# Preparation of the second weights and the stores of finished pair rows on GpSimd's DMA queue, splits in 512-column pieces

## The chip, the cores and the metric

One Trainium2 chip, one core. The time is device microseconds of that core for the whole program, the median of several runs of the same build. TensorE (PE) multiplies, VectorE (DVE), ScalarE (ACT) and GpSimd (POOL) do the elementwise work, and transfers between HBM and the on-chip memory are issued from three queues: SyncE's (SP), ScalarE's (ACT) and GpSimd's (POOL).

## The reference

Linear attention over 8 batches, 8 heads, 576 rows and 64 columns, then two feed-forward layers on the 4608 x 512 result:

```
q_s = softmax over columns of q;  k_s = softmax over rows of k
kv  = k_s^T v;  x = q_s kv                      # x: 4608 x 512
h   = x @ w_in;  x = max(0.01 * h, h) @ w_out           # 512 -> 2048 -> 512
h   = max(x @ w1, x @ w2, x @ w3);  out = h @ w_out      # 512 -> 768 -> 512
```

The weights arrive as 8-byte floats; the result is 4-byte floats.

## The kernel before

**Numbers.** Every multiplied matrix is kept as a high and a low part (two 4-byte tiles), and each product is three matmuls: high x high, high x low, low x high. A split is one ACT copy (the high part) and one DVE subtraction (the low part).

**Stages.** The 4608 rows are nine chunks of 512. Chunks 0 to 2 go through attention and the first layer in the ordinary way (to about 340 us; the attention of the later chunks is prepared beside it and goes on to about 640 us). Chunks 3 to 8 are taken as three pairs, with seven block products in place of eight (Winograd's form of Strassen's scheme), from about 340 to 900 us: for each pair, eight turns `t` make the hidden rows and add up the left half of the output (`out_a(i, 0, ...)`), then a second half of the pair adds up the right side (`out_a(i, 1, ...)`), and in each half the last step evicts four finished accumulators (`store_pair`, L941). The second layer does the same for four pairs, from about 900 us to the end.

**What runs beside the pairs.** The second layer's weights are prepared during the first layer's pairs: nine `ahead_unit`s (L270) and three `ahead_out`s (L304). Each loads two 512 KB blocks of 8-byte weights (L277, L310), converts them (`convert_ahead`, begins with an ACT `Abs` at L254), makes sums of quarters, splits (`split_ahead`, L263) and stores eight 256 KB parts (L222, L301) or two 512 KB blocks (L327). The first layer's weights are stored again in parts during the first 300 us (`stage_a`, L673; `sums_a`, L688). `background(step)` advances all of these a stage at a time between the matmuls of the pairs. Attention of the later chunks loads k, v and q on POOL's queue (L394, L439, L498) and takes the column maximum there (L437).

**What sets the order.** Each engine and each queue works strictly in order. A scheduler places the instructions by its own estimate of when each can begin, except those given to `pin` (`tc.keep_in_program_order`): pinned instructions of an engine keep the order in which the program was written. SP's queue carries the pairs' weight loads (`group` from `stream_in`, L858; `outw` from `stream_out`, L870), which are pinned too.

**The finished rows.** `store_pair` copies one accumulator to an `st` tile on ACT (L943) and stores its two halves with two 128 KB transfers that ACT itself issues (L945): four accumulators, eight stores per half of a pair, 48 in all. The four `st` buffers are shared with the snapshots of the pairs' products (`snap_a`, L965).

Of the kernel before, what the change touches and what calls it, by code (L numbers as in the profile page):

```python
# [9 lines left out]
F32R = mybir.dt.float32r  # L10
U32 = mybir.dt.uint32
I64 = mybir.dt.int64
AF = mybir.ActivationFunctionType
ALU = mybir.AluOpType
# [5 lines left out]
N = 512  # L20
# [14 lines left out]
H = N // 2  # L35
# [5 lines left out]
BEGUN = (0, 0, 0, 2, 3, 5, 7, 9, 11, 13, 15, 17, 19, 21, 23, 25)  # L41
# [29 lines left out]
def tile_kernel(ctx: ExitStack, tc: tile.TileContext, q, k, v, wa, wb, out):  # L71
# [12 lines left out]
    nc = tc.nc  # L84
# [6 lines left out]
    MA = wa.shape[0]  # L91
# [14 lines left out]
    def psum():  # L106
        return ps.tile([P, N], F32, tag="ps", name="ps")
# [10 lines left out]
    for i in range(4):  # L118
        z = slice(32 * i, 32 * i + 32)
# [18 lines left out]
    x2 = {t: dp.tile([P, KDM, N], F32, name=f"x2_{i}") for i, t in enumerate(turns)}  # L138
# [5 lines left out]
    pin = tc.keep_in_program_order  # L144
# [64 lines left out]
    CYCLE = len(USES) * NU  # L209

    stream = dp.tile([P, CYCLE + 3, 2, H], F32, name="stream")
    lone = [dp.tile([P, 2, H], F32, name=f"lone{i}") for i in range(NU)]
    ready_out = [dp.tile([P, 2, 2, N], F32, name=f"wo{t}") for t in range(MB // 2)]

    def place(part, u):

        return (u + (part in LATE)) % NU * len(USES) + USES.index(part)

    def to_stream(u, t, part):

        i = place(part, u)
        pin(nc.sync.dma_start(stream[:, i], t))  # L222
        if i < 3:
            pin(nc.sync.dma_start(stream[:, CYCLE + i], t))

    def sums_of_quarters(quarters, sums):
        a11, a12, a21, a22 = (quarters[:, i] for i in range(4))
        s2, s4, s1, s3 = (sums[:, i] for i in range(4))
        pin(nc.vector.tensor_tensor(s1, a21, a22, op=ALU.add))
        nc.vector.tensor_tensor(s2, s1, a11, op=ALU.subtract)  # L230
        nc.vector.tensor_tensor(s3, a11, a21, op=ALU.subtract)
        nc.vector.tensor_tensor(s4, a12, s2, op=ALU.subtract)
# [29 lines left out]

    def split_ahead(hi, z):  # L263

        pin(nc.scalar.activation(hi.bitcast(F32R), z, AF.Copy))
        pin(nc.vector.tensor_tensor(z.bitcast(F32R), z, hi, op=ALU.subtract))  # L266

    def two_rooms(t):
        return a_room(), a_room()

    def ahead_unit(u):

        t, j = UNITS[u]
        room, more = two_rooms(t)
        raw = room.bitcast(wb.dtype)[:, : 2 * N]
        for half in range(2):
            pin(nc.sync.dma_start(raw[:, half * N : half * N + N], wb[2 * t + half, j // 2, :, j % 2]))  # L277
        yield
        yield
        hi, whole = more[:, : 2 * N], more[:, 2 * N :]  # L280
        if wb.dtype == I64:
            for left in convert_ahead(raw, hi):
                if left is None:
                    yield
            nc.vector.tensor_tensor(whole, hi, left, op=ALU.add)
        else:
            nc.vector.tensor_copy(whole, raw)
        yield
        hi_sums, sums = room[:, : 2 * N], room[:, 2 * N :]
        sums_of_quarters(*(z.rearrange("p (b n) -> p b n", n=H) for z in (whole, sums)))  # L290
        yield
        split_ahead(hi, whole)
        split_ahead(hi_sums, sums)
        yield
        yield
        quarters, sums = (z.rearrange("p (h b n) -> p b h n", h=2, n=H) for z in (more, room))
        for i, part in enumerate(PARTS[:4]):
            if part in USES:
                to_stream(u, quarters[:, i], part)
            else:  # L300
                pin(nc.sync.dma_start(lone[u], quarters[:, i]))  # L301
        for i, part in enumerate(PARTS[4:]):
            to_stream(u, sums[:, i], part)

    def ahead_out(t):

        room, more = two_rooms(t)
        raw = room.bitcast(wb.dtype)[:, : 2 * N]
        for m in range(2):
            pin(nc.sync.dma_start(raw[:, m * N : m * N + N], wb[2 * t + m, 1, :, 1]))  # L310
        yield
        yield
        hi, z = more[:, : 2 * N], more[:, 2 * N :]
        if wb.dtype == I64:
            for left in convert_ahead(raw, z):
                if left is None:
                    yield
            nc.vector.tensor_tensor(z, z, left, op=ALU.add)
        else:
            nc.vector.tensor_copy(z, raw)  # L320
        yield
        split_ahead(hi, z)
        yield
        yield
        both_parts = more.rearrange("p (h m n) -> p m h n", h=2, m=2)
        for m in range(2):
            pin(nc.sync.dma_start(ready_out[t][:, m], both_parts[:, m]))  # L327

    wB = {}

# [343 lines left out]
    def stage_a(m):  # L674

        w = tiles[m].bitcast(F32)
        nc.sync.dma_start(stream_out[:, m], w[:, :, 1])
        i = m // 2 * len(AUSES)
        quarters = w[:, :, 0].rearrange("p h (b n) -> p b h n", n=H)
        for b in range(2):  # L680
            if m % 2 == 0:
                nc.sync.dma_start(stream_in[:, i + AUSES.index(("a11", "a12")[b])], quarters[:, b])
            elif b == 1:
                nc.sync.dma_start(stream_in[:, i + AUSES.index("a22")], quarters[:, b])
        yield
# [63 lines left out]

    def ahead_units():  # L750
        for m in range(MA):
            yield max(BEGUN[m] + 3, 8), stage_a(m)
        for t in range(MA // 2):
            yield (30, 34, 38, 42, 49, 53, 57, 61)[t], sums_a(t)
        for u, at in enumerate((66, 75, 84, 97, 105, 112, 119, 122, 128)):
            yield at, ahead_unit(u)
        for t, at in enumerate((92, 114, 131)):
            yield at, ahead_out(t)
        for c, at in enumerate((CONV * MA + len(APAIRS) * 2 * MA + 30, CONV * MA + len(APAIRS) * 2 * MA)):
            yield at, join(c)  # L760

    waiting = [u for c in range(2, NC) for u in plan_units(c)] + list(ahead_units())
    waiting.sort(key=lambda u: u[0])
    live = []
# [117 lines left out]
    for turn in turns:  # L882
        c = turn[0]
# [57 lines left out]
    def store_pair(i, side, f, acc):  # L941
        st = gp.tile([P, N], F32, tag="st", name="st", bufs=4)
        nc.scalar.activation(st, acc, AF.Copy)  # L943
        for at, c in enumerate(APAIRS[i]):
            pin(nc.scalar.dma_start(x2[c, 0, MA][:, f, side * H : side * H + H], st[:, at * H : at * H + H]))  # L945

    def out_a(i, side, t, f, pairs, ms=(0, 1)):

# [211 lines left out]
    for i in range(len(APAIRS)):  # L1160
# [6 lines left out]
        for t in range(MA // 2):  # L1167
# [4 lines left out]
            a, c = psum(), psum()  # L1172
# [176 lines left out]
```

## Time and profile before

| | us |
|---|---|
| three runs | 1459.7, 1455.17, 1457.37 |
| median | 1457.37 |
| the profiled execution | 1457.88 |
| its span | 1456.1 |
| PE busy | 1398.8 (96% of the span) |
| DVE, ACT, POOL busy | 874.2, 671.1, 90.2 |

A busy PE is not one at full speed: a matmul of 512 columns starts every 0.227 us when nothing holds it and the granted clock is full, and every 0.43 us at half of it. So lost time is found by counting matmuls in a stretch, not by the busy share alone.

### The profile page before, as it was taken

To read this page: it belongs to the slowest core of one execution; us is meant where nothing else is said; L and a number is where in the kernel's file an instruction comes from. 1 tells how busy PE (TensorE), PEld (TensorE's weight loads), DVE (VectorE), ACT (ScalarE), POOL (GpSimd) and SP (SyncE) were. 2 spreads that over 40 slices of the span, in tenths; PEclk is the share of its full clock that TensorE was granted. 3 is DMA by queue.
4 is the path that set the end of the run, shared out by engine and by line. 5 is a ranking of instruction groups with operands and counts; after the bars stand their busy time and mean duration, and the time that the engine had idled before them with its cause. 6 is when DMAs were issued, how large, how long until landed. Compare 5 with 4: busy or idle time off the path is not lost.

```text
span 1456.1 us, 18203 instructions
## 1 busy us (share of the span) xinstructions
PE 1398.8 (96%) x6624; PEld 1135.5 (78%) x6624; DVE 874.2 (60%) x1407; ACT 671.1 (46%) x1361; POOL 90.2 (6%) x162
## 2 busy tenths in 40 slices
PE   6999999999999899998999959999999999999998
PEld 4688867887888687886888837888888888888887
DVE  8888978965687856755566624356356444535311
ACT  6756857744675636644354433223223323323211
POOL 1000212200111100000000000001000000000000
PEclk9999999999999999999999979999999999999999
DMA  9468764526988839668768796754484664364510
GB/s 371 151 243 297 260 233 148 194 98 240 353 288 316 310 138 339 250 249 324 287 231 329 285 378 217 267 188 166 167 312 157 223 253 160 123 253 150 204 51 37
DMA packets 118809, 336.39 MB, mean 231 GB/s; under 512 B 11584, under 2 KB 59456, under 8 KB 96704
## 3 DMA queue, kind: packets, MB, share of 16 engines
q1 hardware_dynamic: 99904, 290.01, 54.5%
q0 software_dynamic: 9600, 34.73, 7.2%
q10 hardware_dynamic: 9216, 10.49, 2.1%
q8 instruction: 52, 0.85, 0.2%
q14 instruction: 37, 0.30, 0.1%
HBM read 256.80 MB, written 78.38 MB: 230 GB/s over the span
## 4 chain that ended last, share of the span: by engine, by line
PE 88%; DMA 4%; DVE 3%; ACT 2%; issue 2%; SPq 1%; ACTq 0%; POOL 0%; DVEq 0%; POOLq 0%
PE ps L847 39%; PE acc L620 33%; PE ps L620 12%; PE ps L448 1%; PE ps L572 1%; DMA wo<-wo 1%; DMA outw<-stream_out 1%; DMA wo<-room 1%; PE ps L552 1%; DMA spare<-in_q_dram 1%; DMA lone<-room 0%; SPq L222 0%; DMA vt<-in_v_dram 0%; DMA stream<-room 0%; DVE room L266 0%
## 5 line engine op out<-in xcount | busy, mean ns | idle before, releaser
L847 PE MATMUL ps<-op,group 128*128 128x512 f32 x1512 | 352.1, 389 | 0.7 <-ACT snap L1068 0.7
L847 PEld LDWEIGHTS ps<-op,group 128*128 128x128 f32 x1512 | 283.7, 188 | 60.0 <-ACT snap L1068 1.1
L620 PE MATMUL acc<-ghi,outw 128*128 128x512 f32 x768 | 258.6, 404 | 27.4 <-ACT st L943 21.6
L847 PE MATMUL ps<-opA,group 128*128 128x512 f32 x1008 | 250.1, 393 | 2.2 <-ACT snap L968 2.1
L847 PEld LDWEIGHTS ps<-opA,group 128*128 128x128 f32 x1008 | 188.5, 188 | 44.1 <-ACT snap L968 3.8
L620 PEld LDWEIGHTS acc<-ghi,outw 128*128 128x128 f32 x768 | 147.8, 194 | 62.7 <-ACT st L943 24.1
L620 PE MATMUL acc<-glo,outw 128*128 128x512 f32 x384 | 153.5, 400 | 3.5 <-DVE glo L641 3.4
L620 PE MATMUL acc<-wo,h 128*128 128x512 f32 x558 | 135.4, 389 | 0.0
L620 PE MATMUL acc<-ghi,w 128*128 128x512 f32 x384 | 127.9, 395 | 0.7 <-ACT st L650 0.7
L620 PE MATMUL ps<-xhi,w 128*128 128x512 f32 x384 | 126.0, 394 | 1.2 <-ACT g L894 0.8
L1068 ACT ACTIVATE snap<-ps 128x512 f32<-128x512 f32 x108 | 61.7, 596 | 134.5 <-PE ps L847 134.1
L620 PEld LDWEIGHTS acc<-wo,h 128*128 128x128 f32 x558 | 104.7, 188 | 21.8
L1083 DVE TENSOR_TENSOR snap<-snap,ps 128x512 f32<-128x512 f32 x72 | 49.2, 685 | 110.5 <-ACT snap L1068 91.5
L641 DVE TENSOR_TENSOR glo<-g,ghi 128x512 fp32r<-128x512 f32 x102 | 69.7, 687 | 67.5 <-ACT ghi L640 67.1
L620 PEld LDWEIGHTS acc<-glo,outw 128*128 128x128 f32 x384 | 74.1, 193 | 20.9 <-DVE glo L641 5.3
L620 PEld LDWEIGHTS ps<-xhi,w 128*128 128x128 f32 x384 | 71.9, 188 | 17.7 <-ACT g L894 1.2
L640 ACT ACTIVATE ghi<-g 128x512 fp32r<-128x512 f32 x102 | 63.6, 630 | 46.2 <-DVE g L1272 27.3
L620 PEld LDWEIGHTS acc<-ghi,w 128*128 128x128 f32 x384 | 71.6, 188 | 17.0 <-ACT st L650 1.4
L641 DVE TENSOR_TENSOR glo<-right,ghi 128x512 fp32r<-128x512 f32 x48 | 33.1, 689 | 82.6 <-ACT ghi L640 82.4
L1092 ACT ACTIVATE h<-best 128x512 fp32r<-128x512 f32 x48 | 30.3, 631 | 100.2 <-DVE best L1085 99.8
L620 PE MATMUL acc<-glo,w 128*128 128x512 f32 x192 | 75.8, 395 | 0.5 <-DVE glo L641 0.5
L620 PE MATMUL ps<-xlo,w 128*128 128x512 f32 x192 | 75.1, 391 | 0.1
(171 smaller groups left out, 1843.1 us busy)
## 6 DMA issues: line engine op xcount, KB each, us to landing
group<-stream SPq DMA_DIRECT2D x62, 1024.0 KB, 5.9
outw<-stream_out SPq DMA_DIRECT2D x48, 1024.0 KB, 9.1
group<-stream_in SPq DMA_DIRECT2D x42, 1024.0 KB, 8.0
stream<-room SPq DMA_DIRECT2D x66, 256.0 KB, 3.2
raw<-in_wa_dram SPq DMA_DIRECT2D x16, 1024.0 KB, 7.4
room<-in_wb_dram SPq DMA_DIRECT2D x24, 512.0 KB, 7.5
x<-st SPq DMA_DIRECT2D x40, 256.0 KB, 3.4
stream_out<-w SPq DMA_DIRECT2D x16, 512.0 KB, 3.4
```

Of the source, the lines that this page charges most:

```text
L448: nc.tensor.matmul(acc[z, : D + 1], lhsT=ke[:, r, z], rhs=vt[:, r, h], start=r == 0, stop=r == RK - 1)
L552: nc.tensor.matmul(both(xps, c0, c1), lhsT=plain_of(b, hp), rhs=halves(qf, c0, c1), start=True, stop=True)
L572: nc.tensor.matmul(both(xps, c0, c1), lhsT=a, rhs=halves(y, c0, c1), start=i == 0, stop=i == 2)
L620: nc.tensor.matmul(acc, lhsT=l, rhs=r, start=first and i == 0, stop=last and i == 2)
L640: nc.scalar.activation(hi[:, z], g[:, z], AF.Copy)
L641: nc.vector.tensor_tensor(lo[:, z], g[:, z], hi[:, z].bitcast(F32), op=ALU.subtract)
L847: nc.tensor.matmul(bank, lhsT=l, rhs=r, start=fresh and first, stop=last, skip_group_check=not fresh)
L1068: nc.scalar.activation(t, bank, AF.Copy)
L1083: nc.vector.tensor_tensor(snap, snap, bank, op=ALU.add)
L1092: nc.scalar.activation(h[:, m, 0], g, AF.Copy)
```

## The change

Seven transfers or groups of them change queue: the loads of the second weights' blocks, the stores of their parts (`to_stream`, `lone`, `ready_out`), which SP issued, and the stores of finished pair rows, which ACT issued. All go to POOL, pinned. `split_ahead` works on 512 columns at a time instead of 1024. The first of the four sums in `sums_of_quarters` is no longer pinned. `stage_a` begins two steps later.

```diff
     def to_stream(u, t, part):
         i = place(part, u)
-        pin(nc.sync.dma_start(stream[:, i], t))
+        pin(nc.gpsimd.dma_start(stream[:, i], t))
         if i < 3:
-            pin(nc.sync.dma_start(stream[:, CYCLE + i], t))
+            pin(nc.gpsimd.dma_start(stream[:, CYCLE + i], t))
...
-        pin(nc.vector.tensor_tensor(s1, a21, a22, op=ALU.add))
+        nc.vector.tensor_tensor(s1, a21, a22, op=ALU.add)
...
     def split_ahead(hi, z):
-        pin(nc.scalar.activation(hi.bitcast(F32R), z, AF.Copy))
-        pin(nc.vector.tensor_tensor(z.bitcast(F32R), z, hi, op=ALU.subtract))
+        for i in range(0, z.shape[1], N):
+            h, l = hi[:, i : i + N], z[:, i : i + N]
+            pin(nc.scalar.activation(h.bitcast(F32R), l, AF.Copy))
+            pin(nc.vector.tensor_tensor(l.bitcast(F32R), l, h, op=ALU.subtract))
...
-            pin(nc.sync.dma_start(raw[:, half * N : half * N + N], wb[2 * t + half, j // 2, :, j % 2]))
+            pin(nc.gpsimd.dma_start(raw[:, half * N : half * N + N], wb[2 * t + half, j // 2, :, j % 2]))
...
-                pin(nc.sync.dma_start(lone[u], quarters[:, i]))
+                pin(nc.gpsimd.dma_start(lone[u], quarters[:, i]))
...
-            pin(nc.sync.dma_start(raw[:, m * N : m * N + N], wb[2 * t + m, 1, :, 1]))
+            pin(nc.gpsimd.dma_start(raw[:, m * N : m * N + N], wb[2 * t + m, 1, :, 1]))
...
-            pin(nc.sync.dma_start(ready_out[t][:, m], both_parts[:, m]))
+            pin(nc.gpsimd.dma_start(ready_out[t][:, m], both_parts[:, m]))
...
         for m in range(MA):
-            yield max(BEGUN[m] + 3, 8), stage_a(m)
+            yield max(BEGUN[m] + 5, 8), stage_a(m)
...
-            pin(nc.scalar.dma_start(x2[c, 0, MA][:, f, side * H : side * H + H], st[:, at * H : at * H + H]))
+            pin(nc.gpsimd.dma_start(x2[c, 0, MA][:, f, side * H : side * H + H], st[:, at * H : at * H + H]))
```

Lines behind L264 have a number two higher in the changed kernel.

The first place is ACT at the end of the last pair's first half, before the change. `st<-acc` is the eviction of an accumulator, `x_14`, `x_15` are the rows being stored, `ghi<-right` the split of the next hidden tile of the second half:

```order
L943 ACTIVATE st<-acc 128x512 x2
L945 DMA x_14_137<-st 128x256
L945 DMA x_15_138<-st 128x256
L945 DMA x_14_137<-st 128x256
L945 DMA x_15_138<-st 128x256
L943 ACTIVATE st<-acc 128x512 x2
L640 ACTIVATE ghi<-right 128x512
L945 DMA x_14_137<-st 128x256
L945 DMA x_15_138<-st 128x256
L945 DMA x_14_137<-st 128x256
L945 DMA x_15_138<-st 128x256
```

and the same place in the changed kernel:

```order
L966 ACTIVATE right<-snap 128x512
L945 ACTIVATE st<-acc 128x512 x4
L642 ACTIVATE ghi<-right 128x512 x3
L809 ACTIVATE op<-side 128x512 x2
L642 ACTIVATE ghi<-right 128x512
```

The four evictions now stand one behind the other, and no DMA issue stands between an eviction and the splits of the second half.

The second place is SP's queue around the end of the middle pair's first half, before the change (`stream` and `lone` are the prepared parts, `room` the tile of a unit of preparation):

```order
L870 DMA outw<-stream_out 128x2048
L222 DMA stream<-room 128x2x256 x2
L301 DMA lone_143<-room 256x1x256
L222 DMA stream<-room 128x2x256 x5
L870 DMA outw<-stream_out 128x2048
L277 DMA room<-in_wb_dram 128x512 x2
L870 DMA outw<-stream_out 128x2048 x6
```

Of these, the changed kernel leaves `outw` and `group` loads on SP. The others stand on POOL's queue, in this order (`x_12`, `x_13` are the middle pair's rows):

```order
L500 DMA qt<-in_q_dram 128x512
L312 DMA room<-in_wb_dram 128x512 x2
L279 DMA room<-in_wb_dram 128x512 x2
L329 DMA wo_149<-room 128x2x512 x2
L947 DMA x_12_135<-st 128x256
...
L947 DMA x_13_136<-st 128x256
L222 DMA stream<-room 128x2x256 x2
L303 DMA lone_143<-room 256x1x256
L222 DMA stream<-room 128x2x256 x5
L279 DMA room<-in_wb_dram 128x512 x2
```

The eight row stores come ahead of the parts of unit 3, and the load of the next unit's weights (the last row) comes behind both.

The third place is ACT in the second half of the middle pair, where that load is first used (`L254 room<-room` is the `Abs` that begins a conversion). Before:

```order
L640 ACTIVATE ghi<-right 128x512
L254 ACTIVATE room<-room 128x1024
L640 ACTIVATE ghi<-right 128x512
L807 ACTIVATE opA<-side 128x1024
L968 ACTIVATE snap<-ps 128x512
L640 ACTIVATE ghi<-right 128x512
```

In the changed kernel, from the evictions on:

```order
L945 ACTIVATE st<-acc 128x512 x4
L642 ACTIVATE ghi<-right 128x512 x3
L809 ACTIVATE opA<-side 128x1024 x2
L970 ACTIVATE snap<-ps 128x512
L642 ACTIVATE ghi<-right 128x512
L966 ACTIVATE g<-snap 128x512
L642 ACTIVATE ghi<-right 128x512 x3
L809 ACTIVATE opA<-side 128x1024 x2
L254 ACTIVATE room<-room 128x1024
```

The conversion begins behind seven splits of the second half, where it began behind two.

## Rows read from the trace of the kernel before

**Rows 1.** The page: busy time, share, instructions; then the chain that ended last.

```profile
PE 1398.8 (96%) x6624; PEld 1135.5 (78%) x6624; DVE 874.2 (60%) x1407; ACT 671.1 (46%) x1361; POOL 90.2 (6%) x162
...
PE 88%; DMA 4%; DVE 3%; ACT 2%; issue 2%; SPq 1%; ACTq 0%; POOL 0%; DVEq 0%; POOLq 0%
```

**Rows 2.** Busy time by stretch; columns as in the first line.

```profile
core 0: us, PE busy (x) PEld busy (x) DVE busy (x) ACT busy (x) POOL busy (x), PEclk, DMA share, GB/s
478.00:498.00 20.00, 14.46 (x61) 10.44 (x56) 14.99 (x27) 13.81 (x32) 2.34 (x4) 0.83 0.98 346
660.00:690.00 30.00, 25.12 (x93) 19.16 (x92) 14.79 (x19) 13.46 (x21) 0.00 (x0) 0.89 0.95 350
838.00:888.00 50.00, 29.96 (x106) 22.36 (x106) 20.84 (x33) 16.99 (x32) 0.00 (x0) 0.80 0.88 327
950.00:1000.00 50.00, 50.00 (x223) 41.39 (x222) 26.39 (x42) 14.38 (x25) 4.99 (x10) 1.00 0.50 169
```

**Rows 3.** The chain in the second layer: start us, us, what.

```profile
953.90 19.04 PE ps L847 x84
```

**Rows 4.** Who PE and ACT waited for: us in total, times, longest.

```profile
PE acc L620 <- ACT st L943: 21.6, 4, 15.2
...
ACT st L943 <- DMA x<-st: 4.4, 1, 4.4
...
ACT ghi L640 <- DMA outw<-stream_out: 6.9, 1, 6.9
...
ACT st L943 <- DMA outw<-stream_out: 16.2, 1, 16.2
```

**Rows 5.** ACT's timeline at two pair ends: start us, us, instructions, [idle before].

```profile
667.42 1.08 ACT L943 ACTIVATE st<-acc 128x512 f32<-128x512 f32 x2 [0.76 <-PE acc L620]
...
842.84 1.09 ACT L943 ACTIVATE st<-acc 128x512 f32<-128x512 f32 x2 [1.68 <-PE acc L620]
846.90 13.21 ACTq L945 DMA_DIRECT2D x<-st  x4
860.15 1.08 ACT L943 ACTIVATE st<-acc 128x512 f32<-128x512 f32 x2 [16.23 <-DMA outw<-stream_out]
```

**Rows 6.** ACT's store issues: duration ns min/median/max, first and last start.

```profile
L945 ACTq DMA_DIRECT2D x<-st x48: 326/362/1192, 483.2 to 921.0; - x48
```

**Rows 7.** SP's `outw` issues (start us, us); their size and median landing, 838 to 888.

```profile
816.85 0.33 SPq L870 DMA_DIRECT2D outw<-stream_out  x1
...
835.65 1.39 SPq L870 DMA_DIRECT2D outw<-stream_out  x2
...
844.95 3.75 SPq L870 DMA_DIRECT2D outw<-stream_out  x4
...
outw<-stream_out SPq DMA_DIRECT2D x5, 1024.0 KB, 14.1
```

**Rows 8.** PE in 478 to 498 us, by shape: busy us, mean ns, idle before.

```profile
L620 PE MATMUL acc<-ghi,outw 128*128 128x512 f32 x27 | 11.3, 490 | 4.7 <-ACT st L943 4.0 <-ACT ghi L640 0.8
L620 PE MATMUL acc<-glo,outw 128*128 128x512 f32 x12 | 5.8, 481 | 0.8 <-DVE glo L641 0.8
...
L448 PE MATMUL ps<-vt,ke 128*64 128x65 f32 x16 | 0.6, 222 | 0.0
```

**Rows 9.** POOL's issues and its reduction: busy us, mean ns, idle before.

```profile
L437 POOL PARTITION_ALL_REDUCE mx<-mx x24 | 21.3, 886 | 252.8 <-PE acc L620 127.4 <-DVE mx L436 104.8 <-DVE qsm L537 15.0
L498 POOL DMA_DIRECT2D qt<-in_q_dram x28 | 15.6, 557 | 185.2 <-DVE qf L558 62.9 <-ACT qhi L562 28.6 <-ACT qf L546 20.9
```

**Rows 10.** Transfers of the whole run: KB each, median us to landing.

```profile
stream<-room SPq DMA_DIRECT2D x66, 256.0 KB, 3.2
...
x<-st ACTq DMA_DIRECT2D x48, 128.0 KB, 7.3
...
joined<-xf POOLq DMA_DIRECT2D x8, 256.0 KB, 4.9
```

**Rows 11.** The weight loads, all 18 of one line: landing us min/median/max.

```profile
DMA to landing us min/median/max: 3.8/6.5/13.5
```

**Rows 12.** Conversions and splits of the preparation: busy us, mean ns, idle before.

```profile
L265 ACT ACTIVATE room<-room 128x1024 fp32r<-128x1024 f32 x21 | 21.3, 1048 | 2.2 <-DVE room L232 2.0
L254 ACT ACTIVATE room<-room 128x1024 f32<-128x1024 f32 x12 | 13.6, 1130 | 2.7 <-ACT right L964 1.0 <-DMA wo<-room 0.9 <-DMA room<-in_wb_dram 0.7
...
L266 DVE TENSOR_TENSOR room<-room 128x1024 fp32r<-128x1024 f32 x21 | 25.0, 1220 | 1.9 <-ACT room L265 1.8
L231 DVE TENSOR_TENSOR room<-room 128x256 f32<-128x256 f32 x17 | 7.1, 418 | 1.7 <-DMA room<-wi 1.6
```

**Rows 13.** Splits of the pairs' hidden rows, 512 columns, ACT and DVE.

```profile
L641 DVE TENSOR_TENSOR glo<-g,ghi 128x512 fp32r<-128x512 f32 x102 | 69.7, 687 | 67.5 <-ACT ghi L640 67.1
...
L640 ACT ACTIVATE ghi<-g 128x512 fp32r<-128x512 f32 x102 | 63.6, 630 | 46.2 <-DVE g L1272 27.3
```

**Rows 14.** The stretch 200 to 250 us, columns as in rows 2.

```profile
200.00:250.00 50.00, 45.72 (x262) 35.09 (x260) 39.99 (x71) 32.45 (x83) 10.39 (x16) 1.00 0.43 140
```

## The prediction

> **What bounds the kernel now.** I read the page first: PE is busy for 96% of the span and is 88% of the chain that ended last [rows 1]. So a change pays only where PE stands still or runs slowly. Next I looked for those places by counting matmuls per stretch. Undisturbed, 84 matmuls of 512 columns take 19.04 us, 0.227 us each [rows 3], and from 950 to 1000 us PE makes 223 in 50 us at a granted clock of 1.00 [rows 2]. Three stretches stand out, each the end of a pair's first half:
>
> - 478 to 498 us: 61 matmuls, 16 of them narrow ones worth 0.6 us [rows 2, 8]. The other 45 need 10.2 us, so 20 - 10.8 = 9.2 us are lost.
> - 660 to 690 us: 93 matmuls need 21.1 us, 8.9 us are lost.
> - 838 to 888 us: 106 need 24.0 us, 26.0 us are lost.
>
> Together 44.1 us. Part is idle time, part the clock: granted 0.83, 0.89 and 0.80 in these stretches [rows 2], that is, some of each at 1.2 instead of 2.4 GHz right after PE had stood idle.
>
> Then the waits: PE waited 21.6 us in four waits for ACT's evictions `st` at L943, the longest 15.2 [rows 4]. And ACT waited at the same places not for PE but for DMA: 16.2 us, 6.9 and 4.4 [rows 4]. ACT's evictions read no DMA result. The timeline shows what it is: after two evictions at 842.84 ACT issues four stores, and these four issues spread over 13.21 us, to 860.11, though one takes 0.36 us [rows 5, 6]; only then do the other two evictions run, at 860.15. The wait before them ended with the landing of an `outw` transfer, SP's [rows 5]. So an issue on ACT is held back until some earlier transfer of SP has landed (that the two share a limited number of transfers in flight is my inference), and PE's accumulators wait behind it, since ACT is in order.
>
> **The change part by part.**
>
> Row stores, 48 issues from ACT to POOL. ACT loses 48 x 0.36 = 17 us of issue time, and the evictions and splits behind them no longer wait for SP's landings. In the changed order the four evictions follow each other. They need four `st` buffers, whose last users are snapshots consumed by then, so they end 4 x 0.55 us after the accumulators (two take 1.09 us, rows 5). Gain: the 44.1 us, less what a pair's end costs anyway. I take that from the first one: 0.8 us for `ghi` and 0.8 for `glo` [rows 8], 1.6 us, three times: 5 us. The data for the resumed work is there: the last pair's second half uses one `outw` tile in 24 matmuls, 5.4 us, and its first three tiles were issued at 816.85 and 835.65 [rows 7]. The fourth is in the group issued from 844.95 on, landing at a median of 14.1 us [rows 7], about 859; PE, going on at 845.5, wants it at 845.5 + 16.3 = 862. Thin, but enough, and the others of that group were issued within 3.75 us.
>
> Preparation's 24 loads and 81 stores, from SP to POOL. With the row stores POOL issues 153 more transfers at 0.56 us [rows 9]: 86 us in some 480 us, in which POOL is mostly waiting. SP no longer waits for a split before its next `outw`; PE waits for no `outw` now, so this gives nothing by itself. The cost is POOL's order. Behind a store that waits for its split stand the attention's k, v and q loads and the reduction. Their waits on POOL are long already, 185.2 us for q alone [rows 9], and their results are used tens of microseconds later; I put this at nothing. What covers it is that slack; without it a pair's operands would come late. The weight loads have less. In the middle pair's second half the chain is: eight row stores from 667 us [rows 5], eight part stores, 16 x 0.56 = 9 us, to 676; the last part lands 3.2 to 7.3 us later [rows 10] (its tile is the next unit's room), so the load starts at 680 to 684 and lands 6.5 us later [rows 11], 686 to 690. The `Abs` that reads it stands behind seven splits of the second half, two of which run at once and each further one after 12 matmuls, 2.7 us: 669 + 5 x 2.7 = 683. ACT then waits 3 to 7 us; the splits run two tiles ahead, which covers 2.7. I take 3 us of PE. The first pair's second half has the same build: 3 us more. The other ten loads are issued in places that are no later than now, or their `Abs` moves back with them. Bounds for all twelve: nothing, to 13.5 - 2.7 = 10.8 us each, 130 us; I stay near the median landing, since today's waits of `Abs` for DMA are 1.6 us in all [rows 12].
>
> How fast POOL's queue lands pieces of 1 KB from a tile no row shows. The nearest are 3.2 us for the same stores on SP, 7.3 for the row stores on ACT and 4.9 for full rows on POOL [rows 10]; all three lie in the chain above. The longest of them in place of the middle moves the 6 us to about 9, the shortest to 3.
> The Trainium skill (SBUF — State Buffer, the section on SBUF's two separate sides) has a rule against this step: GpSimd writes the descriptors of its own transfers, and a VectorE instruction in a two-port mode locks it out of the port, so that a transfer of about 0.62 us measured about 3.1. The conversions contain such VectorE instructions. By that page's figures it would be an estimated 2.5 us for a transfer that meets one, and late loads (below) would be likelier. The trace's issues on POOL average 0.56 us with VectorE 60% busy [rows 1, 9], which does not show it.
>
> Splits of 512 columns. ACT: 42 x 0.630 - 21.3 = +5.2 us; DVE: 42 x 0.687 - 25.0 = +3.9 us [rows 12, 13], spread over 360 us. ACT is 46% and DVE 60% busy [rows 1], and a waiting split of the pairs now stands behind 0.63 instead of 1.05 us. Net on PE: nothing, within 1 us either way.
>
> First weights later, first sum unpinned. SP's order of the first 70 transfers does not change, but the sums of quarters move some 25 us forward on DVE. PE idles 50 - 45.72 = 4.3 us from 200 to 250 us [rows 14], which may go (-4.3). On the other side a sum now may stand on DVE before its data has landed: 1.6 us in two waits now [rows 12], at twice that size for eight units +13. I take +2.
>
> Sum: -44.1 + 5 + 6 + 2 = -31 us. The profiled execution took 1457.9 us (span 1456.1), 0.5 above the median of the runs. 1457.9 - 31 = 1427.
>
> **Rivals.**
>
> The transfers themselves are the bound. For it: the DMA engines are busy for 0.98, 0.95 and 0.88 of the three stretches [rows 2]. If those bytes must land before PE can go on, a stretch shrinks by no more than its free share: 0.4 + 1.5 + 6 = 8 us, and the time is 1450. Against it: most of these bytes are loads ahead of need, and PE's waits name ACT and not `outw` [rows 4].
> The Trainium skill (DMA: Bandwidth & Descriptors, "Issuing engines are not separate DMA queues") says just this: all issuing engines share the same 16 DMA engines, and a second issuer saves only issue time. The shares above agree; rows 5 speak for more, since there the issue itself stood still.
>
> Late weight loads, slower than before. One POOL queue in program order carries stores that wait for splits, and loads behind them; where a load lands more than 2.7 us after its `Abs` has come up on ACT, ACT stops and with it evictions, splits and PE, as ACT's DMA issues do today. It needs many of the twelve to be late, not two. At one median landing each, 12 x (6.5 - 2.7) = 46 us in place of my 6: 1427 + 40 = 1467. The turning point is about 37 us of such waits. For it: some loads are no further ahead than their landing already now, with two waits of `Abs` for DMA [rows 12]. Against it: the changed order puts several `Abs` later by the same delay.
>
> **How the numbers follow.** The forecast, 1427, own range 1414 to 1442 (the bounds of the loads and of the sums): 0.68. Transfers as the bound, 1450: 0.17. Late loads, 1467: 0.15. A measurement of this kernel tells about 0.3%, 4.4 us, from no change. The forecast is all faster; of the second case two thirds; the third leaves a little on the same side. Faster 0.79, same 0.08, slower 0.13. For 8 in 10 the range leaves out the late loads above 1456 and a little below: 1411 to 1456.
>
> **What would show it.** Right: at the three pair ends ACT's evictions run four in a row, no wait of `st` for DMA over 2 us, the granted clock in those stretches near 1.00, and 200 matmuls and more in the 50 us from the last one. Late loads would show as waits of ACT L254 for `room<-in_wb_dram`, the transfers' bound as waits of PE for `outw` or of ACT for an `st` buffer. Wrong altogether if the three stretches close and as much idle time turns up from 200 to 340 us, or if ACT's evictions wait for `x<-st` on POOL's queue.

## The result

The changed kernel took 1446.05 us (median of 7 runs, 1436.12 to 1448.02), the kernel before in the same comparison 1457.96: a ratio of 0.9899, 95% interval [0.987, 0.9927]. It is faster by 11.9 us, where 31 were forecast. The time lies outside the forecast's own range, 1414 to 1442, and inside the wider one, 1411 to 1456. The ratios here and below are of the means of the runs; by them the gain is 14.7 us, since the changed kernel's seven runs fall into two groups, 1436 to 1441 and 1446 to 1448. The profiled execution of the changed kernel took 1440.55 us (span 1438.8, 17.3 less than before). It belongs to the faster group; what the other runs did differently no profile here shows. The lines L943, L945 and L620 of the kernel before are L945, L947 and L622 here.

Page of the changed kernel, busy time, for [rows 1]:

```profile
PE 1392.8 (97%) x6624; PEld 1132.3 (79%) x6624; DVE 876.8 (61%) x1428; ACT 673.9 (47%) x1382; POOL 188.6 (13%) x315
```

PE's busy time fell by 6 us for the same instructions, which I read as clock given back, and its idle time by 11. Where, the stretches show. First the changed kernel, the stretches of [rows 2, 14] and three new ones, the ends of the first two pairs' *second* halves and a place between:

```profile
core 0: us, PE busy (x) PEld busy (x) DVE busy (x) ACT busy (x) POOL busy (x), PEclk, DMA share, GB/s
478.00:498.00 20.00, 17.54 (x107) 13.35 (x106) 19.01 (x35) 15.40 (x35) 7.68 (x11) 1.00 0.82 288
...
530.00:570.00 40.00, 36.35 (x168) 28.44 (x167) 17.17 (x33) 17.39 (x37) 10.65 (x17) 0.96 0.68 240
660.00:690.00 30.00, 29.65 (x130) 23.78 (x129) 16.59 (x20) 14.35 (x22) 8.65 (x14) 1.00 0.84 299
690.00:710.00 20.00, 17.43 (x70) 13.92 (x69) 11.09 (x13) 5.96 (x8) 2.58 (x4) 0.91 0.64 230
710.00:750.00 40.00, 32.86 (x135) 26.34 (x134) 15.78 (x26) 14.89 (x25) 12.69 (x20) 0.91 0.80 287
...
838.00:888.00 50.00, 47.94 (x209) 38.39 (x208) 32.33 (x49) 23.75 (x42) 13.16 (x21) 1.00 1.03 413
...
200.00:250.00 50.00, 46.02 (x259) 34.65 (x258) 40.93 (x75) 32.49 (x83) 9.20 (x15) 1.00 0.63 200
```

And the kernel before in the three new ones:

```profile
530.00:570.00 40.00, 38.78 (x184) 30.76 (x183) 16.36 (x29) 20.25 (x40) 0.54 (x1) 1.00 0.63 228
...
690.00:710.00 20.00, 20.00 (x89) 16.39 (x88) 15.46 (x19) 8.24 (x11) 0.00 (x0) 1.00 0.51 181
710.00:750.00 40.00, 39.89 (x175) 32.36 (x174) 18.66 (x27) 16.88 (x28) 0.00 (x0) 1.00 0.78 278
```

The last pair's first half (838 to 888) makes 209 matmuls for 106: 103 x 0.227 = 23.4 us won. The middle pair's (660 to 690) makes 130 for 93: 8.4 won. Then the other side: 530 to 570 makes 16 fewer (3.6 us lost), 690 to 710 19 fewer (4.3), 710 to 750 40 fewer (9.1). In each of the three the clock is below 1.00 as well, after PE had stood idle.

The first pair's end needs shapes, since narrow matmuls of the attention mix in. From 478 to 518 us the wide ones, before:

```profile
L620 PE MATMUL acc<-ghi,outw 128*128 128x512 f32 x63 | 23.1, 436 | 4.7 <-ACT st L943 4.0 <-ACT ghi L640 0.8
L620 PE MATMUL acc<-glo,outw 128*128 128x512 f32 x31 | 13.6, 439 | 0.8 <-DVE glo L641 0.8
L847 PE MATMUL ps<-opA,group 128*128 128x512 f32 x24 | 6.9, 395 | 0.0
```

and after:

```profile
L622 PE MATMUL acc<-ghi,outw 128*128 128x512 f32 x64 | 21.5, 405 | 1.4 <-ACT st L945 1.4
L622 PE MATMUL acc<-glo,outw 128*128 128x512 f32 x32 | 12.6, 394 | 0.0
L849 PE MATMUL ps<-opA,group 128*128 128x512 f32 x33 | 9.9, 439 | 2.8 <-ACT snap L970 2.4 <-DVE opA L810 0.4
```

129 for 118: 2.5 us won, and the idle time has moved from `st` to `snap`. In all 23.4 + 8.4 + 2.5 - 3.6 - 4.3 - 9.1 = 17.3, the difference of the two profiled spans.

What stands behind the new losses is in the waits of the changed kernel (us in total, times, longest):

```profile
PE acc L622 <- ACT st L945: 12.2, 5, 7.1
...
PE ps L849 <- ACT snap L970: 3.5, 3, 2.4
...
ACT st L945 <- DMA x<-st: 13.5, 2, 8.2
...
ACT room L254 <- issue: 8.4, 3, 4.2
...
ACT snap L970 <- DMA x<-st: 7.1, 2, 6.2
```

Before, ACT waited for `outw`, a transfer that it doesn't read [rows 4]. That row is gone. Now it waits for `x<-st` (before, `st` had 4.9 us of that): for its own buffers, which the row stores still hold. ACT's timeline in the changed kernel at five places:

```profile
510.98 0.60 ACT L970 ACTIVATE snap<-ps 128x512 f32<-128x512 f32 x1 [6.16 <-DMA x<-st]
...
701.20 1.12 ACT L254 ACTIVATE room<-room 128x1024 f32<-128x1024 f32 x1 [4.20 <-issue]
...
726.61 0.60 ACT L945 ACTIVATE st<-acc 128x512 f32<-128x512 f32 x1 [0.73 <-PE acc L622]
727.10 0.59 ACT L970 ACTIVATE snap<-ps 128x512 f32<-128x512 f32 x1
727.58 0.60 ACT L945 ACTIVATE st<-acc 128x512 f32<-128x512 f32 x1
730.01 0.60 ACT L970 ACTIVATE snap<-ps 128x512 f32<-128x512 f32 x1 [1.82 <-PE ps L849]
738.80 0.60 ACT L945 ACTIVATE st<-acc 128x512 f32<-128x512 f32 x1 [8.20 <-DMA x<-st]
...
850.91 2.03 ACT L945 ACTIVATE st<-acc 128x512 f32<-128x512 f32 x4
```

At 850.91, the last pair's first half, four evictions stand in a row, as forecast. At 726 they don't: a second half's evictions alternate with the snapshots of the next pair, and both take `st` buffers in a rotation of four. The third eviction reuses the buffer of the first, written 12 us earlier and not stored yet. POOL's timeline says why the store is late:

```profile
480.33 0.75 POOL L222 DMA_DIRECT2D stream<-room  x1 [5.27 <-DVE room L268]
481.08 0.75 POOL L224 DMA_DIRECT2D stream<-room  x1
481.82 0.72 POOL L222 DMA_DIRECT2D stream<-room  x1
489.47 0.72 POOL L224 DMA_DIRECT2D stream<-room  x1 [6.92 <-PE acc L622]
...
547.21 2.23 POOL L947 DMA_DIRECT2D x<-st  x4 [14.46 <-ACT st L945]
...
723.68 1.46 POOL L222 DMA_DIRECT2D stream<-room  x2 [3.68 <-issue]
725.13 1.12 POOL L279 DMA_DIRECT2D room<-in_wb_dram  x2
727.51 0.55 POOL L947 DMA_DIRECT2D x<-st  x1 [1.25 <-ACT st L945]
732.17 1.08 POOL L947 DMA_DIRECT2D x<-st  x2 [4.11 <-issue]
```

At the middle pair's second half the first row store goes out at 727.51, behind two part stores and two weight loads; the next only at 732.17, after a wait that the profile can only call "issue". By the trace's records the part store of 723.68 had landed at 731.86, the weight loads at 736.77 and 738.02, the row stores at 738.38 and 738.69. ACT's eviction starts at 738.80.

At 555 us ACT waits 5.35 us in the same way for a store that hasn't landed, but here no preparation stands ahead of it: POOL had issued nothing for 14.46 us when four row stores went out from 547.21 on. They landed at 554.75 to 555.75, beside an `outw` load of SP (issued 546.18, landed 554.93), and the DMA engines were busy for 0.87 to 0.94 of the time from 545 to 551 us. That the shared engines made these stores late is the nearest reading. One run below agrees: in loads_sp the same four stores land within 2.3 us, at a DMA share of 0.40 from 540 to 550.

At 480 three part stores go out at once, and the fourth at 489.47, after the first had landed at 489.13.

### The profile page after: what moved, and what is told of

Its sections match the earlier page's. It is cut to its first block, busy times and chain, and to the rows that moved or that the text cites. A ratio compares the mean times of both kernels' runs of the same rounds, so it can differ in the third digit from the quotient of the medians.

```text
span 1438.8 us, 18331 instructions
## 1 busy us (share of the span) xinstructions
PE 1392.8 (97%) x6624; PEld 1132.3 (79%) x6624; DVE 876.8 (61%) x1428; ACT 673.9 (47%) x1382; POOL 188.6 (13%) x315
## 4 chain that ended last, share of the span: by engine, by line
PE 85%; DVE 5%; DMA 4%; ACT 3%; issue 2%; POOL 1%; SPq 0%; ACTq 0%; DVEq 0%; POOLq 0%
PE ps L849 39%; PE acc L622 32%; PE ps L622 11%; DMA x<-st 2%; PE ps L450 1%; PE ps L574 1%; PE ps L554 1%; DMA spare<-in_q_dram 1%; POOL stream L222 1%; DVE glo L643 0%; DMA room<-in_wb_dram 0%; DMA stream_in<-room 0%; ACT qo L514 0%; DVE mx L438 0%; DVE side L814 0%
## 5 line engine op out<-in xcount | busy, mean ns | idle before, releaser
L622 PE MATMUL acc<-ghi,outw 128*128 128x512 f32 x768 | 252.3, 396 | 15.4 <-ACT st L945 12.2
L622 PEld LDWEIGHTS acc<-ghi,outw 128*128 128x128 f32 x768 | 145.4, 190 | 49.2 <-ACT st L945 15.0
L622 PE MATMUL acc<-glo,outw 128*128 128x512 f32 x384 | 151.3, 394 | 1.0 <-DVE glo L643 1.0
L622 PE MATMUL acc<-wo,h 128*128 128x512 f32 x558 | 135.6, 389 | 0.0
L622 PE MATMUL acc<-ghi,w 128*128 128x512 f32 x384 | 127.2, 395 | 0.0
L622 PE MATMUL ps<-xhi,w 128*128 128x512 f32 x384 | 125.9, 394 | 1.2 <-ACT g L896 0.8
L622 PEld LDWEIGHTS acc<-wo,h 128*128 128x128 f32 x558 | 104.7, 188 | 21.8
L622 PEld LDWEIGHTS acc<-glo,outw 128*128 128x128 f32 x384 | 72.9, 190 | 16.8 <-DVE glo L643 1.9
L622 PEld LDWEIGHTS ps<-xhi,w 128*128 128x128 f32 x384 | 72.0, 188 | 17.9 <-ACT g L896 1.2
L622 PEld LDWEIGHTS acc<-ghi,w 128*128 128x128 f32 x384 | 71.5, 188 | 15.6 <-ACT ghi L642 0.4
L622 PE MATMUL acc<-glo,w 128*128 128x512 f32 x192 | 75.9, 395 | 1.7 <-DVE glo L643 1.6
L622 PE MATMUL ps<-xlo,w 128*128 128x512 f32 x192 | 75.2, 392 | 0.1
L1081 DVE TENSOR_TENSOR best<-snap,ps 128x512 f32<-128x512 f32 x36 | 24.7, 685 | 79.6 <-PE ps L849 42.1
```

The source lines that it names most:

```text
L622: nc.tensor.matmul(acc, lhsT=l, rhs=r, start=first and i == 0, stop=last and i == 2)
L1081: nc.vector.tensor_tensor(g, snap, bank, op=ALU.add)
```

## The experiments

Theory T at their start: the gain at the first halves is real; part of it is lost because the row stores share POOL's queue with preparation, land late and hold `st`. Rival B: the DMA engines are full, whoever issues. Rival P: the gain comes from preparation leaving SP. All times are medians, beside runs of the kernel before on the same chip. The scheduler writes each kernel's order anew. Only where the descriptor memory alone differs is every engine's order the same; the other edits move instructions as well. Names with `ends` keep the second halves' evictions out of `st`; `room` is a kernel with another descriptor memory.

| kernel | row stores | preparation | us | ratio to before, 95% |
|---|---|---|---|---|
| rows_only | POOL | SP | 1425.03 | 0.9778 [0.9766, 0.9791] |
| prep_back | POOL | SP | 1427.10 | 0.9790 [0.9775, 0.9805] |
| prep_only | ACT | POOL | 1447.03 | 0.9933 [0.9914, 0.9952] |
| prep_only_loads_sp | ACT | parts POOL, loads SP | 1451.61 | 0.9945 [0.9927, 0.9963] |
| second_act | POOL, ACT | POOL | 1444.37 | 0.9914 [0.9900, 0.9929] |
| loads_sp | POOL | parts POOL, loads SP | 1435.83 | 0.9846 [0.9831, 0.9861] |
| loads_sp_room72 | POOL | parts POOL, loads SP | 1433.70 | 0.9824 [0.9810, 0.9838] |
| room72 | POOL | POOL | 1431.36 | 0.9806 [0.9790, 0.9822] |
| room48 | POOL | POOL | 1486.82 | 1.0193 [1.0174, 1.0212] |
| ends_w | POOL | POOL | 1419.74 | 0.9742 [0.9729, 0.9754] |
| ends_small_undone | POOL | POOL | 1424.45 | 0.9765 [0.9746, 0.9785] |
| rows_only_ends | POOL | SP | 1417.42 | 0.9723 [0.9705, 0.9742] |
| prep_back_ends | POOL | SP | 1419.00 | 0.9735 [0.9720, 0.9751] |
| ends_room72 | POOL | POOL | 1414.28 | 0.9706 [0.9691, 0.9721] |

**One half of the move alone.** rows_only is the kernel before with this:

```diff
-            pin(nc.scalar.dma_start(x2[c, 0, MA][:, f, ...], st[...]))
+            pin(nc.gpsimd.dma_start(x2[c, 0, MA][:, f, ...], st[...]))
```

> The kernel before with one edit alone: the row stores on GpSimd's queue; preparation stays on SyncE's. Theory T (the wait moved: on GpSimd's queue the row stores stand behind the part stores and weight loads, land 7 to 11 us after their issue, and so hold the four st buffers that the ends of the second halves need): without the parts on that queue the stores land in 2 to 5 us, ACT waits for x<-st less than 3 us in all, and both the gain at the first halves' ends (about 33 us) and the second halves stay: 1425 to 1436 us. Rival B (the DMA engines are full at these places, whichever queue carries the bytes): the stores land as late as in the changed kernel, 13 us of waits for x<-st remain, about 1446. Rival P (the gain comes from preparation leaving SyncE): about 1457, as before.

1425.03: T's time; B (1446) and P (1457) are far off. But T's signs came only in part. At the middle pair's second half the row stores land 5.7 to 7.4 us after their issue, with nothing else on POOL's queue and the DMA engines busy for 1.02 of the time from 705 to 713 us. ACT waits 4.5 us for an `st` buffer, where T said less than 3, and PE 3.5 us, where the changed kernel's waits 7.1:

```profile
ACT st L943 <- DMA x<-st: 4.5, 1, 4.5
```

So about half of the loss at this place comes with the row stores' move alone, without any preparation on POOL. prep_back comes from the other end, the changed kernel with its six preparation issues back on `nc.sync`:

> The changed kernel with all of preparation's transfers back on SyncE's queue; the row stores stay on GpSimd's, the splits of 512 and the later first weights stay. Theory T: the row stores land within 5 us, so the loss at the second halves' ends goes, as in the kernel that moved only the row stores (1425.0), less what the small parts give: 1419 to 1427. If the small parts are worth nothing: 1424 to 1427. Rival (preparation on GpSimd's queue is a gain beside the row stores): 1440 or more.

1427.10, 19 us faster than the changed kernel (16 by the ratios). ACT waits 4.4 us for `x<-st`, at the same place as in rows_only. One stretch, with the DMA engines busy all the time and PE undisturbed:

```profile
690.00:710.00 20.00, 20.00 (x90) 16.58 (x89) 4.99 (x8) 4.38 (x7) 0.00 (x0) 1.00 1.00 373
```

So the row stores' move is the gain (-31 to -33), and moving preparation along with them costs 16 to 19. prep_back and rows_only differ by the three small parts of the change (splits of 512, first weights later, first sum not held in order); 2 us lie within the spread of their runs.

**Preparation alone.** prep_only undoes the row stores' move in the changed kernel:

> The changed kernel with the row stores back on ACT; preparation stays on GpSimd's queue. Theory T: ACT's issues are held again until transfers of SyncE have landed, less often, since the part stores are no longer among those counted together: ACT issues of the last pair's first half again spread over several us; 1448 to 1458. Rival P (preparation leaving SyncE is the gain): 1440 to 1446. Rival B: as the changed kernel, 1446, since the bytes are the same.

1447.03: 11 us faster than before, a microsecond above what P gave and a microsecond below what T gave; the time alone decides nothing. With preparation off SP fewer of ACT's issues are held (counted below). But PE stands for 11.2 us from 832 on for another reason, in ACT's timeline:

```profile
842.08 1.12 ACT L254 ACTIVATE room<-room 128x1024 f32<-128x1024 f32 x1 [14.94 <-issue]
```

This is the prediction's late weight load: its `Abs` waits for a load issued at 830.45, landed at 842.01. The next kernel put the loads back on SP:

> The changed kernel with the row stores on ACT's queue (1447.0) and now the 24 weight loads on SyncE's queue too; only the part stores stay on GpSimd's. With the row stores on ACT and the loads on GpSimd's queue, PE stands still for 11.6 us at 832, while ACT's Abs waits 13 us for a weight load issued at 830 (landing 842). Theory L (late weight loads cost where the scheduler places the Abs early): this standstill goes, 1433 to 1438. Rival (the load is late because the DMA engines are full with the side, outw and part transfers of that time, whoever issues it): it lands about 840 again, 1444 to 1449.

1451.61: theory L's time did not come, nor its rival's (1444 to 1449). That late `Abs` is gone, and in its place, at 858, stands the old wait of before:

```profile
854.90 10.66 ACTq L947 DMA_DIRECT2D x<-st  x4
865.61 0.60 ACT L945 ACTIVATE st<-acc 128x512 f32<-128x512 f32 x1 [10.25 <-DMA wo<-wo]
```

More transfers on SP, more holding on ACT. This also settles the inference on which the forecast's gain rested. The records of the kernel before, in the stretch of [rows 5], name the semaphore that each transfer counts on; SP and ACT together use eight in turn. ACT's four issues, and the transfer eight places earlier on the same semaphore:

```
ACT x<-st issued   eight earlier: issued, what        landed
846.90             837.82 SP side<-x                  846.82
849.76             839.45 SP side<-x                  849.74
854.91             843.84 SP wo<-room                 854.83
859.78             845.71 SP outw<-stream_out         859.76
```

Each issue follows that landing by 0.02 to 0.08 us. So what the two queues share, as far as these records show, is the eight semaphores. Of all 48 issues of row stores in the kernel before, 19 begin within 0.12 us after the landing of the transfer before them on their semaphore; in prep_only 2 of 48 do, in prep_only_loads_sp 7.

**Row stores of the second halves on ACT.**

```diff
-            pin(nc.gpsimd.dma_start(x2[...
+            pin((nc.gpsimd, nc.scalar)[side].dma_start(x2[...
```

> The changed kernel with the row stores of the second halves alone on ACT's queue, those of the first halves on GpSimd's. Theory T: at the second halves' ends PE loses about what it lost before (0.7 and 2.7 us for 11.5 and 6.8), the first halves' ends stay as changed: 1431 to 1437. Rival (ACT's issues are held wherever they stand, because SyncE's transfers land late at these ends too): ACT issues of 3 us and more at 550 and 730 us, 1444 to 1450.

1444.37, outside T's 1431 to 1437 and in the rival's range, though not in the rival's way: none of the 24 issues on ACT begins right after a landing on its semaphore. The second halves' ends did improve (720 to 760 us loses 3.4 for 9.8, counted as the excess of each matmul's start-to-start time over 0.227). But in this kernel's order two late `Abs` came up, in ACT's timeline, with PE idle for 4.1 and 9.8 us:

```profile
695.59 1.12 ACT L254 ACTIVATE room<-room 128x1024 f32<-128x1024 f32 x1 [5.75 <-issue]
...
841.77 1.12 ACT L254 ACTIVATE room<-room 128x1024 f32<-128x1024 f32 x1 [13.55 <-issue]
```

**The buffers instead of the queue.** ends_w leaves every transfer of the changed kernel on its queue and frees `st`:

```diff
     def store_pair(i, side, f, acc):
-        st = gp.tile([P, N], F32, tag="st", name="st", bufs=4)
+        if side == 1 and f == 0:
+            ends[i] = wp.tile([P, KDM, N], F32, tag="w", name="ends")
+        st = ends[i][:, f] if side == 1 else gp.tile([P, N], F32, tag="st", name="st", bufs=4)
```

> The changed kernel, but the four evictions at the end of each second half go into one buffer of 8 KB from the weights' pool in place of four st buffers; the transfers stay as they are. Theory T: the waits of ACT for x<-st at 555 and 739 us (5.4 and 8.2) go, PE loses 10 to 15 us less at the second halves' ends: 1431 to 1437. Rival B: the next wait is for data (outw, group), PE stands as long: 1444 to 1448. The buffer taken from the weights could make a load late; that would be a PE wait for outw or group.

1419.74: 26 us less than the changed kernel (23 by the ratios), more than T's 10 to 15. Two stretches, where the kernel before made 184 and 175:

```profile
530.00:570.00 40.00, 40.00 (x196) 33.02 (x195) 19.39 (x38) 20.98 (x48) 9.37 (x15) 1.00 0.70 243
...
710.00:750.00 40.00, 39.34 (x174) 32.27 (x173) 17.94 (x29) 17.36 (x30) 12.38 (x20) 1.00 0.84 307
```

The bytes are the same and the queue too, so rival B falls here as a bound on PE. Against the changed kernel (168 and 135 matmuls) the two stretches win 67 x 0.227 = 15.2 us. What exceeds T's number is mostly the late `Abs` of 701, which the new order doesn't have (690 to 710 us makes 90 matmuls for 70), and the first pair's end. On the same buffers, preparation on SP:

> The kernel before with two edits: the row stores on GpSimd's queue, and the evictions of each second half in one buffer of the weights' pool; preparation stays on SyncE's queue. If moving preparation to GpSimd's queue is worth something beside the row stores' move, this is slower than the same buffers with preparation moved (1419.7): 1422 to 1428. If it is worth nothing once st is free, 1417 to 1421. If it costs (late weight loads), under 1417.

> The same, and the second halves' evictions in one buffer of the weights' pool. The two kernels with that buffer took 1417.4 (preparation on SyncE's queue, without the small parts) and 1419.7 (on GpSimd's, with them); undoing the small parts cost the latter 4.7. If the parts add up: 1411 to 1415. If the 4.7 came from where the scheduler then put one Abs, and not from the parts: 1416 to 1421.

1417.42 and 1419.00: with `st` free, preparation's queue is worth nothing that these runs tell apart. And the small parts undone:

> The kernel with the second halves' evictions in one buffer of the weights' pool (1419.7), with three small parts of the change undone: splits of 1024 columns, the first weights' parts two steps earlier, the first sum pinned. Prediction's costing: splits nothing, the other two 2 us of loss in the change, so 1416 to 1421. Rival (the splits of 512 let ACT's evictions in sooner): 1424 or more.

1424.45, 4.7 more than ends_w, 3.4 by the ratios, whose intervals overlap. The time is the one that the rival named. In the profiled execution PE stands for 7.9 us from 825 on, where ACT waits 8.9 us with one `Abs` (829.75) for its weight load. The pair rows_only_ends and prep_back_ends differs by the same parts and shows none of it. I take the 4.7 for that `Abs`, not for the splits; the rival isn't excluded, since it wasn't tried apart.

**The room for descriptors.** One number, every engine's order unchanged:

```diff
-dynamic_dma_scratch_size=1024
+dynamic_dma_scratch_size=1152   (room72)
+dynamic_dma_scratch_size=768    (room48)
```

> The changed kernel with GpSimd's descriptor memory of 1152 bytes a partition in place of 1024. In the changed kernel three part stores in a row are issued within 2.2 us, and the fourth only after the first of them has landed (489.47 after 489.13). Theory R (this memory limits the transfers in flight): now four in a row are issued at once, the row stores behind them land some us sooner, ACT's waits for x<-st shrink from 13 us by a third or more: 1434 to 1441. Rival B (the landings are paced by the DMA engines, which SyncE's loads share): the issues come sooner, the landings do not: 1441 to 1448, waits as in the changed kernel.

> The changed kernel with GpSimd's descriptor memory of 768 bytes a partition in place of 1024; each engine's order of instructions is the same. With 1152 bytes the time fell from 1446 to 1431 and four part stores went out in a row in place of three. Theory R (this memory limits GpSimd's transfers in flight, and that is part of the 19 us lost): now two part stores go out in a row, everything behind them on GpSimd's queue is later, 1455 or more. Rival (the 15 us came from other addresses in the state buffer or from the spread of the runs): three in a row as with 1024, 1431 to 1448.

1431.36 and 1486.82. POOL's timeline at the place where the changed kernel sent three part stores in a row; with 1152 bytes, four:

```profile
479.54 0.75 POOL L222 DMA_DIRECT2D stream<-room  x1 [5.23 <-DVE room L268]
480.29 0.74 POOL L224 DMA_DIRECT2D stream<-room  x1
481.03 0.74 POOL L222 DMA_DIRECT2D stream<-room  x1
481.76 0.73 POOL L224 DMA_DIRECT2D stream<-room  x1
```

with 768, two:

```profile
479.42 0.76 POOL L222 DMA_DIRECT2D stream<-room  x1 [5.27 <-DVE room L268]
480.17 0.74 POOL L224 DMA_DIRECT2D stream<-room  x1
487.89 0.72 POOL L222 DMA_DIRECT2D stream<-room  x1 [6.98 <-issue]
```

Theory R's first half holds: this memory limits POOL's transfers in flight, and the order of every engine is the same in the three kernels. With 768 bytes the late `Abs` alone make ACT wait 46.6 us:

```profile
ACT room L254 <- issue: 46.6, 4, 19.0
```

But R's way was not as I put it, and 1431.36 is below its range. With 1152 bytes ACT's wait for `st` hardly shrank:

```profile
ACT st L945 <- DMA x<-st: 11.9, 2, 6.9
...
ACT snap L970 <- DMA x<-st: 2.7, 2, 1.7
```

What went is the `snap` wait at 511 (7.1 to 2.7 in all) and the loss at 701: compared matmul by matmul, PE gets 4.0 us ahead from 500 to 515 and 3.7 from 700 to 705. Another 1.5 us lie in the first 40, where other kernels with 1024 bytes differ as much from one another; I don't count these. The profiled spans differ by 9.8 us in all; the 14.7 of the medians is more because the changed kernel's profiled execution is one of its faster ones. At 718 the row stores now go out at once, and still land with the weight loads ahead of them, at 727.7 to 728.7 after 727.4.

**Loads or parts.**

> The changed kernel with the 24 weight loads alone back on SyncE's queue; part stores and row stores stay on GpSimd's. In the changed kernel two weight loads issued at 725 us land at 737 and 738, and the first row store of the pair's end, issued behind them at 727.5, at 738.4. Theory T (the row stores land late because of what stands ahead of them on GpSimd's queue): they land by about 732, the wait of ACT for x<-st there falls from 8.2 us to under 4, the late Abs at 701 (4.2 us of ACT, 3.0 of PE) changes too: 1430 to 1438. Rival B (the DMA engines are full then, whoever issues): row stores land about as late, 1441 to 1448.

> The kernel with the weight loads back on SyncE's queue (1435.8) and 1152 bytes of descriptor memory. All preparation back on SyncE's queue gave 1427.1. If the other 9 us that the part stores still cost on GpSimd's queue are the room for descriptors: 1425 to 1430. If they are the order alone (row stores behind part stores) or the bandwidth: 1433 to 1437.

1435.83: the 24 loads are 10 of the 19 us (8 of 16 by the ratios). The first row stores of the middle pair's second half land at 726.8 to 730.1, as T said, and ACT's wait for `st` falls to a quarter:

```profile
ACT st L945 <- DMA x<-st: 3.3, 2, 3.1
```

1433.70: without the loads on the queue more room gives only 2, and the intervals overlap. So the remaining 7 to 9 us are the part stores' order on POOL, the bandwidth, or what the move does to the scheduler's order; which, the runs don't tell.

**The best of it.**

> The changed kernel with the second halves' evictions in one buffer of the weights' pool (1419.7) and 1152 bytes of descriptor memory. If that memory only mattered because late row stores held st: 1418 to 1421. If it also brings weight loads and parts forward (the first pair's end lost 4 us less with it): 1413 to 1417.

1414.28 us, 2.9% faster than before and 2.2% faster than the changed kernel (2.0% by the ratios), with both causes met: room for descriptors, and no `st` buffer behind POOL's queue.

## Why the prediction was wrong

- **The mechanism of the gain was right.** ACT's issues were held by landings of SP, and taking them off ACT closes the first halves of the last two pairs: 23.4 and 8.4 us for 24.4 and 7.3 forecast (26.0 and 8.9, less 1.6 each). rows_only shows it alone, at 1425.
- **The step that failed** is what the row stores cost on POOL's queue, which the sum has at nothing: "They need four `st` buffers, whose last users are snapshots consumed by then". That holds at the first halves, the only place where I had checked it. At the second halves the buffer's last user is an eviction 12 us earlier, whose store hasn't landed. And "The cost is POOL's order. Behind a store that waits for its split stand the attention's k, v and q loads and the reduction", with "I put this at nothing", leaves out the row stores themselves: they stand on the same queue, and they hold `st`. Cost: 3.6 + 9.1 us at the two second halves, and 5.1 at the first pair's end, where 2.5 came for 7.6, mostly because `snap` waited there for the same stores (4 of it came back in room72). Not all of it is the queue's order: at 555 us nothing stood ahead of the stores, and at the middle pair rows_only waits without any preparation on the queue. The buffer is what all of it has in common, and ends_w, which frees it, removes the loss in both second halves.
- **Late loads**, 6 us forecast in two places: 4.3 in one, 690 to 710, where ACT waited 4.2 and PE 2.6, the rest lower clock. The first pair has none. One more `Abs`, at 779, waits 3.8 us and costs PE nothing. As a rival at 1467 the late loads did not come here, though the mechanism is the one that cost most in prep_only and room48.
- **The transfers as the bound** fell at the last pair: 209 matmuls in 50 us at a DMA share of 1.03. That the measured time lies near this rival's 1450 is chance. The Trainium skill (DMA: Bandwidth & Descriptors, "Issuing engines are not separate DMA queues") says that transfers of all issuing engines run on the same 16 DMA engines, and that a second issuer saves only the time of issuing, usually small beside the transfer. POOL's row stores that land beside SP's `outw` at 555 agree with the first. Small the saving was not here, since a held issue held ACT: 48 issues moved gave 31 to 33 us.
- **Sums**, +2: PE's idle time from 200 to 250 us is 4.0 for 4.3; from 250 to 340 us it is 1.8 for 0.7. Together 0.9 of the 2. **Splits**, nothing: they were never tried apart from the other two small parts; of three comparisons of all three parts, two show no difference beyond the spread.

To the forecast's -31.1 (-44.1 + 5 + 6 + 2) these terms add: +12.7 (second halves), +5.1 (first pair's end), -0.1 (the other two first halves), -1.7 (late loads), -1.1 (sums). That gives -16.2, where the profiled spans differ by 17.3; about 1 us isn't placed. The signal named at the end of the prediction, ACT's evictions waiting for `x<-st` on POOL's queue, is what showed.

## What to carry to other kernels

An issue moved to an empty queue is worth what it held up; before moving a second group to the same queue, list what the first group's transfers keep occupied, at every place where such a buffer comes round again. A wait that the profile names after a transfer the engine doesn't read can be a shared limit: look for the transfer whose landing it follows within 0.1 us. Two moves that each help, 33 and 11 us, can give 12 together.

## What the runs showed of the hardware

- POOL's transfers in flight are limited by the descriptor memory: two part stores in a row at 768 bytes, three at 1024, four at 1152, with nothing older of POOL's in flight there by the records. If every store holds the same share, my estimate from these three is that a store of 256 KB holds more than 256 of these bytes (three don't fit 768, four don't fit 1024) and at most 288 (four fit 1152).
- The price of that memory is steep: 256 bytes less cost 41 us, 128 more gave 15 by the medians, 42 and 10 by the profiled spans.
- POOL's row stores of 128 KB, with nothing ahead of them on its queue, land 2.2 us after their issue at a DMA share of 0.40 (loads_sp, 544 us), and 6.8 to 7.5 us after it at 0.87 to 0.94 (the changed kernel, 547 us).
- PE lost clock after each of the new standstills: granted 0.91 to 0.96 over the stretch around them, that is, part of it at 1.2 instead of 2.4 GHz, and 1.00 in the same stretch of ends_w.
